# Unit pipeline of a top-k attention with a feed-forward block: P@V, scores, transpose, sine and gate at other places in each step

## The chip, the cores and the metric

The kernel runs on one core of one Trainium2 chip. The metric is the device time in microseconds (us) of one execution; a span is the same time as the profiler sees it. The engines that appear below are TensorE (PE, with its weight loads as PEld), VectorE (DVE), ScalarE (ACT), GpSimd (POOL) and SyncE (SP, which here only issues transfers).

## The reference

Attention over 8 batches x 8 heads, 576 positions, head size 64, in float32. Each row of scores keeps its 32 largest entries, and only these enter the softmax. The result, with the heads side by side, is the input of a feed-forward layer with 4608 tokens, width 512 and inner width 2048.

```python
scores = scale * np.matmul(q, k.transpose(0, 1, 3, 2))      # q, k, v: (8, 8, 576, 64)
kth = np.partition(scores, -32, axis=-1)[..., -32:-31]
scores = np.where(scores >= kth, scores, -1000000000.0)
scores = scores - np.max(scores, axis=-1, keepdims=True)
attn = np.exp(scores)
attn = attn / (np.sum(attn, axis=-1, keepdims=True) + 1e-09)
x = np.matmul(attn, v)             # then (B, H, S, D) -> (B*S, H*D): (4608, 512)
h = x @ w_in                       # w_in: (512, 2048)
g = h * np.cos(h)
out = g @ w_out                    # w_out: (2048, 512)
```

## The kernel before

The work is cut into 144 **units**: a unit is 128 tokens and one pair of heads (`hp`, 0 to 3). Four units make a **block** of 128 tokens, so there are 36 blocks. A batch has 576 tokens, which is 4.5 blocks; every ninth block therefore lies across two batches, and its units have two parts. The constants are `NP = 4`, `NU = 144`, `NF = 16`, `NC = 4`.

A unit goes through these stages, on different engines: scores (PE), copy out of PSUM (ACT), top-32 by four rounds of MAX8 and MATCH_REPLACE8 (DVE), mask and exponentials (ACT), reciprocal (DVE), normalise (POOL), split of the 32-bit words into two 16-bit halves (POOL), a write of the halves to DRAM and a transposing transfer back (SP), P@V (PE), and a copy to `xT` (ACT). The program is one Python loop; its step `i` emits one stage each of several neighbouring units, and every engine runs its own instructions in the order in which they were emitted. I call one pass of that loop a **step**. The two weight matrices arrive as 64-bit floats and are turned into 32-bit ones on ACT, DVE and POOL during the first steps (`load_weights`, `decode_first` to `decode_third`). Steps 0 to 8 are `early_slot`, 9 to 140 are `slot`, 141 to 144 are `last_slot`.

The feed-forward part of a finished block is woven into the steps in small portions: a block has 8 **first portions** (`ff1`, x @ w_in, 16 matmul instructions each) and 8 **second portions** (`ff2`, g @ w_out, 4 matmul instructions each). For each half block of h the cosine is made by a reduction (POOL), a sine (ACT) and a product called the gate (POOL). Whether a portion may be emitted is decided in Python by counters:

```python
    def can_first():
        if not first:
            return False
        blk, i = first[0]
        if blk["left"] or ff["tick"] < blk["tick"] + 2 or wq["ready"] < (((i + 1) * (256 // blk["w"]) - 1) // FC + 1) * NC:
            return False
        return i % 4 > 0 or ff["live"] + staged() < CHUNKS

    def can_second():
        if not second:
            return False
        blk, i, f = second[0]
        lag = 3 if 5 * NP < ff["now"] < NU - NP else 2
        gated = sum(ff["tick"] >= t + lag for t in blk["gated"])
        return gated * 1024 // blk["w"] >= f + 2 and wq["ready"] >= NC * NF // FC + f + 2

    def feed(n):
        ff["tick"] += 1
        while n > 0 and ff["credit"] >= 1:
            for kind in (ff["kind"], 1 - ff["kind"]):
                if (can_first, can_second)[kind]():
                    break
            else:
                return
            if kind == 0:
                ff1(*first.popleft())
            else:
                ff2(*second.popleft())
            if kind != ff["kind"] or ff["half"]:
                ff["kind"], ff["half"] = 1 - kind, 0
            else:
                ff["half"] = 1
            n, ff["credit"] = n - 1, ff["credit"] - 1
```

The stages that the change moves:

```python
    def write_halves(u):
        rows = u["rows"] = dram.tile([P, 2, 2 * S], U16, tag="rows", name="rows")
        nc.sync.dma_start(out=rows, in_=u.pop("halves"))

    def transposes(u):
        rows = u.pop("rows").rearrange("q h k -> (q h) k")
        pT = u["pT"] = work.tile([P, 2 * NT + 1, P], F32, tag="pT", name="pT", bufs=3)
        words = pT.rearrange("p c q -> p (c q)").bitcast(U16)
        nc.sync.dma_start_transpose(
            out=words.rearrange("p (c q) -> p c q", c=2 * NT + 1), in_=rows
        )

    # ... (cut)

    def take_values(us):
        blk, hp, n = block_of[us[0]["tok"]], us[0]["hp"], len(us)
        if "xT" not in blk:
            blk["xT"] = work.tile([P, NP, P], F32, tag="xT", name="xT", bufs=5)
        nc.scalar.copy(
            out=blk["xT"][:, hp : hp + n].rearrange("p h q -> p (h q)"),
            in_=room[0][:, 0 : n * P],
        )
        blk["left"] -= n
        blk["tick"] = ff["tick"]

    # ... (cut)

    def reduce_second():
        if not fresh or len(fresh[0]) < 3:
            return
        blk, g, x = fresh.popleft()
        if not ff["end"]:
            nc.gpsimd.tensor_tensor(out=x, in0=g, in1=x, op=ALU.subtract)
        waiting.append((blk, g, x, ff["now"], -TWO_PI_BELOW if ff["end"] else TWO_PI_BELOW))

    def sines(least):
        n = sum(c[3] < ff["now"] for c in waiting)
        if n == 0 or (n < least and waiting[0][3] + 2 > ff["now"]):
            return
        for _ in range(n):
            blk, g, x, _, scale = waiting.popleft()
            nc.scalar.activation(out=x, in_=x, func=AF.Sin, bias=halfpi, scale=scale)
            sined.append((blk, g, x))

    def gate(n):
        for _ in range(min(n, len(sined))):
            blk, g, x = sined.popleft()
            eng = nc.vector if ff["end"] else nc.gpsimd
            eng.tensor_tensor(out=g, in0=g, in1=x, op=ALU.mult)
            blk["gated"].append(ff["tick"])
```

The step of the middle of the run. `u` is unit i (top-k), `w` unit i-1 (mask, exponentials), `x` unit i-2 (reciprocal to write), `y` unit i-3 (transpose), `z` a pair of units whose P@V is made:

```python
    def slot(i, u, w, x, y, z):
        if x:
            reciprocal(x)
        if u:
            topk_first(u, w)
            decode_second(2)
        if u:
            topk_round(u, 1)
            topk_round(u, 2)
            topk_round(u, 3)
        if z:
            values(z)
        made = scored.get(i, [])
        if z:
            take_banks()
        else:
            feed(1)
        for m in made:
            scores(m)
        late = len(made) > 0
        if w:
            bounds(w)
            mask(w)
        take_banks()
        if w and late:
            exponentials(w)
        if z:
            take_values(z)
        take_scores(units[i + 1])
        if w and not late:
            exponentials(w)
        for load, b, hp in at_slot.get(i, []):
            load(b, hp)
        load_weights(2)
        if y:
            transposes(y)
        gate(1)
        if x:
            normalise(x)
            split(x)
            write_halves(x)
        feed(2)
        take_banks()
        decode_third()
        decode_first(2)
        reduce_first()
        reduce_second()
        feed(1 if len(made) == 2 else 3)
        if i % 2:
            sines(1)
        elif i < EARLY + 8 or i > LAST - 2:
            sines(2)
```

Which step makes whose scores and loads, and the loop:

```python
    EARLY, LAST = 2 * NP, NU - NP
    scored, last, last_values = {}, {}, {}
    for i, u in enumerate(units):
        two = i % 2 and EARLY + 2 < i < LAST + 2 and len(u["parts"]) == 1
        scored.setdefault(i - 2 if two else i - 1, []).append(u)
        for part in u["parts"]:
            last[part[0], u["hp"]] = i - 2 if two else i - 1
            last_values[part[0], u["hp"]] = i
    at_slot = {}
    order = [(b, hp) for b in range(B) for hp in range(NP)]
    for n in range(NP, len(order)):
        i = last[order[n - 5]] if n >= 5 else 0
        at_slot.setdefault(max(i, NP + 2), []).append((load_qk, *order[n]))
        i = last_values[order[n - 6]] if n >= 6 else 0
        at_slot.setdefault(max(i + 5 - i % 2, NP + 2), []).append((load_v, *order[n]))
    for hp in range(NP):
    # ... (cut)
    for i in range(NU + 1):
        ff["end"] = i >= NU
        ff["credit"] = min(ff["credit"] + 5.0 - 0.9 * len(scored.get(i, [])), 5.3)
        ff["now"] += 1
        wq["ready"] = wq["done"]
        u, w = (units[i - n] if 0 <= i - n < NU else None for n in range(2))
        x, y = (units[i - n] if EARLY <= i - n < LAST else None for n in range(2, 4))
        z = units[i - 5 : i - 3] if i % 2 and EARLY <= i - 5 < LAST else None
        if i <= EARLY:
            early_slot(i, u, w)
        elif i <= LAST:
            slot(i, u, w, x, y, z)
        else:
            last_slot(i, u, w, x, y, z)
    while first or second or full:
        ff["now"] += 1
        # ... (cut)
```

Of the kernel before, what the change touches and what calls it, by code (L numbers as in the profile page):

```python
# [31 lines left out]
def kernel(  # L32
# [16 lines left out]
    NP = H // 2  # L49
# [35 lines left out]
    for i in range(DF // CW):  # L85
        w = consts.tile([P, NC, CW], F32, tag=f"w_in{i}", name=f"w_in{i}")
# [4 lines left out]
    for f in range(NF):  # L91
        w = consts.tile([P, DM], F32, tag=f"w_out{f}", name=f"w_out{f}")
# [3 lines left out]
    ff = {"live": 0, "tick": 0, "now": 0, "credit": 0.0, "end": False, "kind": 0, "half": 0, "open": 0}  # L96
# [58 lines left out]
    units = []  # L155
    for t0 in range(0, B * S, P):
        parts = []
# [8 lines left out]
    NU = len(units)  # L166
# [174 lines left out]
    def reciprocal(u):  # L341
        u["rden"] = small.tile([P, 2], F32, tag="rden", name="rden")
        nc.vector.reciprocal(u["rden"], u.pop("den"))  # L343
# [19 lines left out]
# [11 lines that stand above are left out]
# [17 lines left out]
    def values(us):  # L391


        o = room[0]
        for i, u in enumerate(us):
            pT = u.pop("pT")
            for b, _, rows, r0 in u["parts"]:
                st = pairs[b, u["hp"]]
                r = slice(r0, r0 + rows)
                to = slice(i * P + r0, i * P + r0 + rows)  # L400
                for c in range(NT + 1):
                    for j in range(2):
                        d = slice(j * D, (j + 1) * D)
                        if c < NT:
                            lhsT, rhs = st["v"][:, c, d], pT[:, j * (NT + 1) + c, r]
                        else:
                            lhsT, rhs = st["v_tail"][:, d], pT[:, NT, r]
                        nc.tensor.matmul(o[d, to], lhsT, rhs, start=c == 0, stop=c == NT)  # L408
# [73 lines left out]
    def take_banks():  # L482
        while full:
            take, *what = full.popleft()
            take(*what)
# [30 lines left out]
# [16 lines that stand above are left out]
# [36 lines left out]
    def can_second():  # L568
        if not second:
            return False  # L570
        blk, i, f = second[0]

        lag = 3 if 5 * NP < ff["now"] < NU - NP else 2
        gated = sum(ff["tick"] >= t + lag for t in blk["gated"])
        return gated * 1024 // blk["w"] >= f + 2 and wq["ready"] >= NC * NF // FC + f + 2

# [18 lines that stand above are left out]
# [8 lines left out]
    EARLY, LAST = 2 * NP, NU - NP  # L603
    scored, last, last_values = {}, {}, {}
    for i, u in enumerate(units):
        two = i % 2 and EARLY + 2 < i < LAST + 2 and len(u["parts"]) == 1
        scored.setdefault(i - 2 if two else i - 1, []).append(u)
        for part in u["parts"]:
            last[part[0], u["hp"]] = i - 2 if two else i - 1
# [4 lines that stand above are left out]
        i = last[order[n - 5]] if n >= 5 else 0  # L614
        at_slot.setdefault(max(i, NP + 2), []).append((load_qk, *order[n]))
        i = last_values[order[n - 6]] if n >= 6 else 0
        at_slot.setdefault(max(i + 5 - i % 2, NP + 2), []).append((load_v, *order[n]))

    for hp in range(NP):
        at_slot.setdefault(hp, []).append((load_v, 0, hp))  # L620
# [44 lines left out]
        feed(2)  # L665
        sines(2)

    def slot(i, u, w, x, y, z):
        if x:
            reciprocal(x)  # L670
        if u:
# [3 lines that stand above are left out]
            topk_round(u, 1)  # L675
            topk_round(u, 2)
            topk_round(u, 3)
        if z:
            values(z)
        made = scored.get(i, [])  # L680
        if z:
            take_banks()
        else:
            feed(1)
        for m in made:
            scores(m)


        late = len(made) > 0
        if w:  # L690
            bounds(w)
            mask(w)
# [8 lines that stand above are left out]
        for load, b, hp in at_slot.get(i, []):  # L701
            load(b, hp)
        load_weights(2)
        if y:
            transposes(y)
        gate(1)
        if x:
            normalise(x)
            split(x)
            write_halves(x)  # L710
        feed(2)
        take_banks()
        decode_third()
        decode_first(2)
        reduce_first()
        reduce_second()
        feed(1 if len(made) == 2 else 3)
        if i % 2:
            sines(1)
        elif i < EARLY + 8 or i > LAST - 2:  # L720
            sines(2)

    def last_slot(i, u, w, x, y, z):
        if x:
            reciprocal(x)
        if u:
# [9 lines that stand above are left out]
        if i + 1 < NU:  # L736
            scores(units[i + 1])
        if z:
            take_values(z)
        if i + 1 < NU:  # L740
            take_scores(units[i + 1])
        if y:
            transposes(y)
        if x:
            normalise(x)
            split(x)
            write_halves(x)
        reciprocal(w)
        normalise(w)
        if u:  # L750
            topk_round(u, 2)
            topk_round(u, 3)
        gate(2)
        feed(2)
        transposes_now(w)
# [4 lines that stand above are left out]
        values([w])  # L760
        take_values([w])
        feed(2)
# [10 lines left out]
# [3 lines that stand above are left out]
        ff["now"] += 1  # L776
        wq["ready"] = wq["done"]
        u, w = (units[i - n] if 0 <= i - n < NU else None for n in range(2))
        x, y = (units[i - n] if EARLY <= i - n < LAST else None for n in range(2, 4))
        z = units[i - 5 : i - 3] if i % 2 and EARLY <= i - 5 < LAST else None  # L780
        if i <= EARLY:
            early_slot(i, u, w)
        elif i <= LAST:
            slot(i, u, w, x, y, z)
        else:
            last_slot(i, u, w, x, y, z)
    while first or second or full:
        ff["now"] += 1
        ff["credit"] = 2.0
# [44 lines left out]
```

## Time and profile before

| | |
|---|---|
| time, median of 3 | 1523.82 us (1522.76 to 1524.04) |
| span of the profiled execution | 1521.9 us |
| PE matmul / PE weight load busy | 1417.3 us (93%) / 1020.5 us (67%) |
| DVE busy | 1416.0 us (93%) |
| ACT busy | 1149.2 us (76%) |
| POOL busy | 1102.9 us (72%) |
| mean transfer rate | 139 GB/s |

The table gives each engine's busy time over the whole span. It can't be read as a single limit, because the run has stages: until about 200 us the feed-forward weights are still being decoded, then a long regular middle follows, and from about 1400 us the last units and the feed-forward work that is left. The profile also has a view by stretches of time, a list of waits (who stood idle, and what released it), and a timeline, in which an engine's instructions stand in order with the idle time before each and its releaser. "L465" is line 465 of the kernel; the lines that matter are L304 and L307 (top-k), L465 (first portions), L543 (second portions), L408 (P@V), L220 (scores), L348 and L360 (normalise, split), L365 and L371 (write, transpose), L504 to L513 (reduction), L523 (sine) and L530 (gate).

### The profile page before, as it was taken

How to read it: one execution, taken by the hardware profiler on the slowest of the kernel's cores; microseconds unless marked ns; L12 is line 12 of the kernel's file. 1: busy time of each engine (PE TensorE's matmuls, PEld its weight loads, DVE VectorE, ACT ScalarE, POOL GpSimd, SP SyncE). 2: the span in 40 equal slices, each digit the busy share in tenths (PEclk: the TensorE clock that was granted, in tenths of full speed). 3: DMA queues.
4: the chain of work that ended last, by engine and by line, in shares of the span. 5: the costliest groups of instructions: out<-in, count | busy, mean ns of one | idle time of the engine just before them, and what ended most of it. 6: DMA issues, size and time to landing. Idle time of an engine off the chain costs nothing.

```text
span 1521.9 us, 30207 instructions
## 1 busy us (share of the span) xinstructions
PE 1417.3 (93%) x10360; PEld 1020.5 (67%) x10360; DVE 1416.0 (93%) x4690; ACT 1149.2 (76%) x2322; POOL 1102.9 (72%) x837
## 2 busy tenths in 40 slices
PE   4567798999999999999999999999999999999899
PEld 3365365676777767777777767777777767776774
DVE  7989999999999999999999999999999999999521
ACT  7888766777777778877777777777777777777631
POOL 4777966778777778777777777777777777776500
PEclk6587999999999999999999999999999999999899
DMA  8422364645655555646655456555664455545000
GB/s 265 139 83 83 99 178 135 186 117 175 161 169 132 132 148 164 179 132 156 165 170 132 132 151 168 171 133 152 167 171 132 132 151 158 151 132 132 17 15 14
DMA packets 371753, 212.20 MB, mean 139 GB/s; under 512 B 321296, under 2 KB 337936, under 8 KB 371600
## 3 DMA queue, kind: packets, MB, share of 16 engines
q1 hardware_dynamic: 366192, 200.63, 48.7%
q10 hardware_dynamic: 5408, 9.65, 1.9%
q8 instruction: 81, 1.33, 0.4%
q14 instruction: 72, 0.59, 0.1%
HBM read 45.09 MB, written 87.29 MB: 87 GB/s over the span
## 4 chain that ended last, share of the span: by engine, by line
DVE 74%; PE 12%; ACT 6%; issue 3%; POOL 2%; DMA 2%; SPq 1%; DVEq 0%; ACTq 0%; POOLq 0%
DVE top L304 33%; DVE rest L307 27%; DVE rest L244 11%; PE o L543 5%; PE mm L465 4%; PE rim L408 2%; ACT s L334 1%; DVE top L292 1%; ACT s L326 1%; DVE top L297 1%; DVE w_out L138 1%; PE sc L220 1%; DMA pT<-rows 1%; DVE rden L343 1%; ACT st L127 1%
## 5 line engine op out<-in xcount | busy, mean ns | idle before, releaser
L304 DVE MAX8 top<-rest 128x8 f32<-128x288 f32 (+1 forms) x1656 | 681.2, 460 | 0.0
L465 PEld LDWEIGHTS mm<-xT,w_in 128*128 128x128 f32 x4608 | 536.3, 193 | 83.4 <-ACT g L478 39.8
L465 PE MATMUL mm<-xT,w_in 128*128 128x128 f32 x4608 | 546.9, 277 | 7.4 <-ACT g L478 3.4
L543 PE MATMUL o<-w_out,g 128*128 128x512 f32 x1152 | 532.1, 605 | 11.3 <-POOL g L530 5.6
L307 DVE MATCH_REPLACE8 rest<-top,rest 128x288 f32<-128x288 f32 (+1 forms) x1104 | 494.6, 455 | 0.0
L348 POOL TENSOR_SCALAR s<-s,rden 128x576 f32<-128x576 f32 x288 | 212.7, 750 | 259.1 <-DVE rden L343 259.1
L543 PEld LDWEIGHTS o<-w_out,g 128*128 128x128 f32 x1152 | 209.3, 192 | 232.4 <-issue 210.4
L360 POOL COPY halves<-s 128x2304 uint16<-128x2304 uint16 x132 | 277.7, 2103 | 27.4 <-DMA rows<-halves 19.9
L334 ACT ACTIVATE s<-s,nd 128x576 f32<-128x576 f32 x288 | 219.7, 764 | 0.8
L244 DVE TENSOR_TENSOR rest<-sc,s 128x576 f32<-128x576 f32 x264 | 198.5, 752 | 10.2 <-ACT s L231 2.7
L326 ACT ACTIVATE s<-s,nb 128x576 f32<-128x576 f32 x288 | 205.3, 760 | 0.0
L314 ACT ACTIVATE nb<-top 128x4 f32<-128x4 f32 x144 | 29.6, 206 | 230.2 <-DVE top L297 229.6
L408 PE MATMUL rim<-pT,v 128*64 128x128 f32 (+1 forms) x2560 | 163.1, 272 | 21.5 <-ACT pT L389 13.7
L530 POOL TENSOR_TENSOR g<-g,x 128x1024 f32<-128x1024 f32 x67 | 158.3, 2363 | 22.3 <-ACT nb L314 11.4
L220 PE MATMUL sc<-k,q 64*128 64x448 f32 (+1 forms) x640 | 150.1, 583 | 17.0 <-DMA k<-in_k_dram 9.3
L513 POOL TENSOR_TENSOR x<-g,x 128x1024 f32<-128x1024 f32 x68 | 161.0, 2367 | 5.7
L408 PEld LDWEIGHTS rim<-pT,v 128*64 128x64 f32 x2560 | 134.4, 141 | 38.3 <-ACT pT L389 16.3
L230 ACT COPY s<-sc 128x896 f32<-128x896 f32 x144 | 129.0, 896 | 3.3 <-PE sc L220 3.3
L478 ACT ACTIVATE g<-mm 128x512 f32<-128x512 f32 x144 | 83.7, 583 | 54.3 <-PE mm L465 43.9
L220 PEld LDWEIGHTS rim<-k,q 64*128 64x128 f32 (+1 forms) x640 | 57.3, 180 | 57.8 <-issue 52.7
L523 ACT ACTIVATE x<-x,halfpi 128x1024 f32<-128x1024 f32 x72 | 82.5, 1149 | 6.9 <-DVE x L499 6.1
L523 ACT ACT_TABLE_LOAD x66 | 84.7, 1283 | 1.6 <-ACT ob L553 0.4
(55 smaller groups left out, 1232.0 us busy)
## 6 DMA issues: line engine op xcount, KB each, us to landing
rows<-halves SPq DMA_DIRECT2D x132, 576.0 KB, 3.2
out_dram<-ob ACTq DMA_DIRECT2D x36, 256.0 KB, 2.9
q<-in_q_dram SPq DMA_DIRECT2D x31, 288.0 KB, 3.3
st<-in_moe_w_in_dram SPq DMA_DIRECT2D x16, 512.0 KB, 5.8
v<-in_v_dram SPq DMA_DIRECT2D x32, 256.0 KB, 3.9
st<-in_moe_w_out_dram SPq DMA_DIRECT2D x16, 512.0 KB, 3.6
k<-in_k_dram SPq DMA_DIRECT2D x31, 144.0 KB, 3.4
k<-in_k_dram SPq DMA_DIRECT2D x32, 128.0 KB, 3.8
```

Source lines behind the costliest of these rows:

```text
L220: nc.tensor.matmul(to[r0 : r0 + rows, j, 0 : k1 - k0], st["q"][d, q0 : q0 + rows], st["k"][d, k0:k1], start=True, stop=True,)
L244: nc.vector.tensor_tensor(out=u["rest"][:, :, i * HS : (i + 1) * HS], in0=sc[:, :, 0:HS], in1=s[:, :, HS:S], op=op,)
L304: nc.vector.max(to[:, j], src[:, j])
L307: nc.vector.match_replace(rest[:, j], to[:, j], src[:, j], NEG)
L326: nc.scalar.activation(out=s[:, j], in_=s[:, j], func=AF.Prelu, bias=nb[:, j, 1:2], scale=SCALE, alpha=FAR)
L334: nc.scalar.activation(out=s[:, j], in_=s[:, j], func=AF.Exp, bias=nd[:, j : j + 1], scale=1.0, accum_out=den[:, j : j + 1],)
L348: nc.gpsimd.tensor_scalar(out=s[:, j], in0=s[:, j], scalar1=rden[:, j : j + 1], scalar2=1.0, op0=ALU.mult, op1=ALU.mult,)
L360: nc.gpsimd.tensor_copy(out=halves, in_=s.rearrange("p (k h) -> p h k", h=2))
L408: nc.tensor.matmul(o[d, to], lhsT, rhs, start=c == 0, stop=c == NT)
L465: nc.tensor.matmul(mm[:, at : at + w], w_in[f // FC][:, c, (f % FC) * P : (f % FC + 1) * P], blk["xT"][:, c], start=c == 0, stop=c == NC - 1,)
L523: nc.scalar.activation(out=x, in_=x, func=AF.Sin, bias=halfpi, scale=scale)
L543: nc.tensor.matmul(o, g[:, at : at + P], w_out[f], start=f == 0, stop=f == NF - 1)
```

## The change

The change re-times the stages against each other; it adds no arithmetic and takes none away.

- P@V and the scores of two units were both emitted in odd steps; now both are in even steps. A pair's P@V (units 2k and 2k+1) moves from step 2k+5 to step 2k+4, and one feed-forward portion is emitted ahead of it.
- The transpose of a unit was emitted in the step after its write; now it directly follows the write in the same step.
- The sine was emitted at the end of odd steps; now it stands at the head of odd steps, ahead of the mask of that step.
- The gate was emitted ahead of normalise and split; now it comes behind them.
- The age in ticks that a gate must have before a second portion may use it is 3 from step 12 on, where it was 3 from step 20 on.
- The loads of v are emitted one step earlier, and units of head pair 0 that lie across two batches also get their scores one step earlier.

It is meant to shorten the way of a unit from top-k to the feed-forward part.

```diff
--- before.py
+++ after.py
@@ -570,7 +570,7 @@
             return False
         blk, i, f = second[0]
 
-        lag = 3 if 5 * NP < ff["now"] < NU - NP else 2
+        lag = 3 if 3 * NP < ff["now"] < NU - NP else 2
         gated = sum(ff["tick"] >= t + lag for t in blk["gated"])
         return gated * 1024 // blk["w"] >= f + 2 and wq["ready"] >= NC * NF // FC + f + 2
 
@@ -603,7 +603,7 @@
     EARLY, LAST = 2 * NP, NU - NP
     scored, last, last_values = {}, {}, {}
     for i, u in enumerate(units):
-        two = i % 2 and EARLY + 2 < i < LAST + 2 and len(u["parts"]) == 1
+        two = i % 2 == 0 and EARLY + 2 < i < LAST + 2 and (len(u["parts"]) == 1 or u["hp"] == 0)
         scored.setdefault(i - 2 if two else i - 1, []).append(u)
         for part in u["parts"]:
             last[part[0], u["hp"]] = i - 2 if two else i - 1
@@ -614,7 +614,7 @@
         i = last[order[n - 5]] if n >= 5 else 0
         at_slot.setdefault(max(i, NP + 2), []).append((load_qk, *order[n]))
         i = last_values[order[n - 6]] if n >= 6 else 0
-        at_slot.setdefault(max(i + 5 - i % 2, NP + 2), []).append((load_v, *order[n]))
+        at_slot.setdefault(max(i + 4 - i % 2, NP + 2), []).append((load_v, *order[n]))
 
     for hp in range(NP):
         at_slot.setdefault(hp, []).append((load_v, 0, hp))
@@ -665,7 +665,7 @@
         feed(2)
         sines(2)
 
-    def slot(i, u, w, x, y, z):
+    def slot(i, u, w, x, z):
         if x:
             reciprocal(x)
         if u:
@@ -675,18 +675,19 @@
             topk_round(u, 1)
             topk_round(u, 2)
             topk_round(u, 3)
-        if z:
-            values(z)
         made = scored.get(i, [])
         if z:
             take_banks()
-        else:
-            feed(1)
+        feed(1)
+        if z:
+            values(z)
         for m in made:
             scores(m)
 
 
         late = len(made) > 0
+        if i % 2:
+            sines(1)
         if w:
             bounds(w)
             mask(w)
@@ -701,26 +702,23 @@
         for load, b, hp in at_slot.get(i, []):
             load(b, hp)
         load_weights(2)
-        if y:
-            transposes(y)
-        gate(1)
         if x:
             normalise(x)
             split(x)
             write_halves(x)
-        feed(2)
+            transposes(x)
+        gate(1)
+        feed(1 if len(made) == 2 else 2)
         take_banks()
         decode_third()
         decode_first(2)
         reduce_first()
         reduce_second()
         feed(1 if len(made) == 2 else 3)
-        if i % 2:
+        if i < EARLY + 4 or i == LAST:
             sines(1)
-        elif i < EARLY + 8 or i > LAST - 2:
-            sines(2)
-
-    def last_slot(i, u, w, x, y, z):
+
+    def last_slot(i, u, w, x, z):
         if x:
             reciprocal(x)
         if u:
@@ -739,12 +737,11 @@
             take_values(z)
         if i + 1 < NU:
             take_scores(units[i + 1])
-        if y:
-            transposes(y)
         if x:
             normalise(x)
             split(x)
             write_halves(x)
+            transposes(x)
         reciprocal(w)
         normalise(w)
         if u:
@@ -776,14 +773,14 @@
         ff["now"] += 1
         wq["ready"] = wq["done"]
         u, w = (units[i - n] if 0 <= i - n < NU else None for n in range(2))
-        x, y = (units[i - n] if EARLY <= i - n < LAST else None for n in range(2, 4))
-        z = units[i - 5 : i - 3] if i % 2 and EARLY <= i - 5 < LAST else None
+        x = units[i - 2] if EARLY <= i - 2 < LAST else None
+        z = units[i - 4 : i - 2] if i % 2 == 0 and EARLY <= i - 4 < LAST else None
         if i <= EARLY:
             early_slot(i, u, w)
         elif i <= LAST:
-            slot(i, u, w, x, y, z)
+            slot(i, u, w, x, z)
         else:
-            last_slot(i, u, w, x, y, z)
+            last_slot(i, u, w, x, z)
     while first or second or full:
         ff["now"] += 1
         ff["credit"] = 2.0
```

## The prediction

> **What bounds the kernel now.** I read the page first: busy times, then the 40 slices.
>
> ```profile
> PE 1417.3 (93%) x10360; PEld 1020.5 (67%) x10360; DVE 1416.0 (93%) x4690; ACT 1149.2 (76%) x2322; POOL 1102.9 (72%) x837
> ...
> PE   4567798999999999999999999999999999999899
> DVE  7989999999999999999999999999999999999521
> ```
>
> Two engines are full, but not at the same ends. PE starts slowly and works to the last slice; DVE is full early and empty in the last three slices (a slice is 38 us). The view by stretches (us; then busy PE, PEld, DVE, ACT, POOL with counts, clock, DMA share, GB/s) says the same in numbers:
>
> ```profile
> 500.00:700.00 200.00, 197.77 (x1562) 143.82 (x1560) 198.86 (x695) 159.65 (x322) 155.47 (x116) 1.00 0.55 147
> 1400.00:1450.00 50.00, 44.06 (x305) 32.80 (x300) 30.14 (x81) 33.13 (x71) 25.00 (x21) 0.90 0.18 42
> 1450.00:1522.00 72.00, 68.13 (x345) 44.54 (x343) 13.80 (x13) 13.49 (x20) 0.03 (x1) 1.00 0.04 15
> ```
>
> In the middle a step lasts 9.51 us (reciprocals at 1390.79 and 1400.31 in the timeline) and DVE is busy 99.4% of it: DVE sets the pace there. After 1400 us DVE has little left and PE runs on. So the end is DVE's pace up to step 140 **plus the PE work still open then**. How much is open? The same view for L465 (ff1) and then for L543 (ff2) alone:
>
> ```profile
> 1400.00:1456.00 56.00, 18.65 (x128) 17.84 (x128) 0.91 0.17 42
> 1456.00:1522.00 66.00, 22.40 (x192) 22.38 (x192) 1.00 0.03 12
> ```
> ```profile
> 1400.00:1456.00 56.00, 15.48 (x34) 6.25 (x35) 0.91 0.17 42
> 1456.00:1522.00 66.00, 41.68 (x95) 17.22 (x93) 1.00 0.03 12
> ```
>
> An ff1 portion is 16 instructions, an ff2 portion 4. Open at 1400 us: 320/16 = 20 first and 129/4 = 32 second portions, 52 of 576. Of these 12 and 24 lie after the last P@V (1455.2 us). One portion costs (1518.1 - 1455.2)/36 = 1.75 us of PE there; two take 3.44 to 3.66 us in the middle. Only the last block's 16 must come after its P@V; the other 20 are backlog, 35 us of it. Backlog is what this change can shorten.
>
> **What the Trainium skill says.** "Perfetto Trace Analysis", section Identifying the Most-Contended Engine, warns that matmul busy share isn't a measure of PE's headroom. It agrees here in so far as "busy" PE hides waits: I therefore count PE work in portions. From its section Optimization Strategy I take that a kernel can have several regimes; this one has three. "DMA: Bandwidth & Descriptors", section Two DMAs through the same engine are not ordered, says that a dependent transfer has to wait for the first one's completion semaphore. The trace shows that wait: between 300 and 1395 us, SP's queue stood 238.4 us before transposes for their rows. "ScalarE: Activation LUTs", section What ACT_TABLE_LOAD costs, gives about 1283 ns for a load; the trace has 1283 ns, 66 before sines. The change doesn't alter how often sine and exponentials alternate (once in two steps), so I count nothing for it.
>
> **The change, part by part.**
>
> *P@V one step earlier.* A pair's P@V comes in step 2k+4 instead of 2k+5; a block is ready for ff1 a step, 9.5 us, earlier. The credit rule gives 5.0 - 0.9 per scored unit, capped at 5.3. In both kernels a step with two scored units can emit at most 3 portions (2+1 before, 1+1+1 after), a step with none emits 5; so 8 per two steps in both, which is exactly the demand (16 per block of four steps). PE work of two steps: 8 portions 14.2 us, two P@V 2.4, two scores 2.15, in sum 18.76 us of 19.02 (714.39 to 716.79 to 718.94 us in the timeline, and the four pairs of portions before). So the middle can't go faster, and backlog lost early is never made up: **its size at step 140 is decided in the steps before 32**.
>
> *Sine at the head, gate behind the split.* Before, a reduction emitted in odd step i isn't old enough for the sine at the end of i; it waits until i+2, and its gate until i+3. After, the reduction falls in even step i, the sine at the head of i+1, the gate in i+1. A gate comes about two steps sooner, so ff2 may follow sooner.
>
> *Counting it.* I stepped the counters of `feed` through all steps for both versions (credit, ticks, lag, weight readiness). Portions emitted by the end of a step:
>
> ```
> step      14  17  20  22  26  28  30  32  140
> before    31  40  50  56  72  78  84  92  524
> after     31  40  51  59  75  83  91  99  532
> ```
>
> The count before agrees with the trace (268 + 256 = 524 portions by 1400 us). What the older kernel loses: in step 27 only one portion is emitted, because the gate of the next ff2 is under 3 ticks old and the new block's ff1 isn't ready; in step 30, three instead of five. After, the wider lag costs an empty step 17, but from 18 on every pair of steps gives 8. By 32 the lead is 7, with the different rhythm of step 140 it is 8. Behind the last P@V 28 portions are left instead of 36. Saved: 8 x 1.75 = **14.0 us**. The last steps 141 to 144 (about 55 us, four or five portions each) I leave as they are.
>
> *Transpose issued with its write.* Per unit SP now waits about 3.2 us (median landing of a write) with its queue blocked, then 2.6 us of issue: 6.2 us with the write, of 9.5 us per step. In steps with eight q/k loads (about 4.6 us) that is 10.8, more than a step. From a normal odd step: split ends 3.9 us into it (1.5 normalise, 2.1 split), write landed at 7.1, transpose landed 4.8 us later at 11.9; PE begins an even step 0.8 us before DVE (714.39 against 715.17), then makes a portion (1.8) and the other unit's P@V (1.2), so it reaches that unit's P@V at 9.5 + 2.2 = 11.7. So PE may wait 0.2 us and a few us in load steps. Each shifts PE against DVE once; PE can run about 3.5 us later before the next unit's scores are late. Cost: 0 to 2 us at the end.
>
> *Start of the run.* Here POOL, full with weight decoding, is late:
>
> ```profile
> 186.97 1.47 POOL L348 TENSOR_SCALAR s<-s,rden 128x576 f32<-128x576 f32 x2
> 188.50 2.10 POOL L360 COPY halves<-s 128x2304 uint16<-128x2304 uint16 x1
> ```
> ```profile
> 194.47 2.57 SPq L371 DMA_TRANSPOSE pT<-rows  x1
> ```
>
> This is unit 11, whose reciprocal was at 178.61: normalise begins 8.4 us late, and the transpose, issued at 194.47, lands about 199. Before, its P@V comes in step 15 (198.34 us), just in time. After, it comes in step 14, which PE reaches near 190; POOL does the same work, so it still lands about 199. The scores of unit 15 stand behind that P@V, ready about 201.4, copied by ACT about 202.7; DVE wants them at 197.8. I expect a **DVE stall of about 5 us** once, which moves everything later. Some of the old start's waits (1.97 us of DVE for ACT's copy at 247 us) may go. Net +4 us.
>
> Sum: 1523.8 - 14.0 + 4 = 1513.8; with 0 to 2 us of PE waits, and 1 to 2 us back because P@V of two units leaves the last steps: **1513 us**.
>
> **Rivals.** *ACT's sine becomes a wait of each pair.* Look at one pair of steps (reduction, sine, end of the merge, bounds):
>
> ```profile
> 703.39 2.37 POOL L513 TENSOR_TENSOR x<-g,x 128x1024 f32<-128x1024 f32 x1
> ...
> 704.57 1.15 ACT L523 ACTIVATE x<-x,halfpi 128x1024 f32<-128x1024 f32 x1
> ...
> 707.33 0.18 DVE L297 TENSOR_REDUCE top<-top 128x2 f32<-128x34 f32 x1
> ...
> 707.55 0.21 ACT L314 ACTIVATE nb<-top 128x4 f32<-128x4 f32 x1 [1.83 <-DVE top L297]
> ```
>
> Here the sine is of an older reduction. After, it is the one just made: POOL ends it at 705.76, the sine would end at about 707.0, and the mask needs ACT at 707.5. It fits by half a microsecond; the exponentials of that step ended 0.76 us before DVE's next reciprocal (714.41, 715.17). A POOL delay over about 1.3 us would stall DVE, in each of some 60 pairs: 0.3 us each is 18 us, and the time is 1530. For it: the thin margin. Against: the gate no longer stands ahead of normalise, POOL rests over 3 us in odd steps, and ACT waits 198.4 us for DVE between 300 and 1395 us, 1.7 us each time.
>
> *SP becomes the bound*, if transposes pile up behind loads: each P@V then waits, scores behind it are late, DVE waits too. For it: the 10.8 us of a load step. Against: only three steps of the run load eight, and average SP use is about 7 us of 9.5. It would give 1520 to 1535.
>
> *Nothing is gained*, if PE simply idles where it had worked: then backlog doesn't shrink, and 1524 +- 3 results. Against it stands the count, which the trace of before confirms.
>
> **Range and chances.** The gain from the count alone with no stall at the start gives 1508; with the last steps shorter too, 1504. A stall of 5 us and PE waits give 1515; with the first rival in mild form, 1525. Range 1504 to 1525. Over 2% faster would be under 1493: it needs 17 portions, while only 20 are backlog; 3%. Over 2% slower is over 1554: half a microsecond of DVE per pair; 4%. Within 2%: 93%.
>
> **What would show it.** Right: L465 and L543 together have 28 portions after the last P@V; DVE stays over 99% busy in the middle; one DVE idle of 3 to 6 us for ACT's copy (L231) near 198 us. Wrong: reciprocals in the middle more than 9.55 us apart; DVE waiting for ACT's den (L339) or copy in each pair; P@V waiting for the transfer of pT by tens of us in sum; or as many portions left as before.

## The result and the profile after

The changed kernel takes 1541.92 us (median; 1539.52 to 1551.65) against 1523.29 us: a ratio of 1.0135, 95% interval 1.009 to 1.018. It is slower, by 18.6 us or 1.35%, and lies outside the predicted range.

The page after, the lines that answer to those shown of before (busy times, then tenths busy in 40 slices, each now 38.5 us):

```profile
PE 1419.2 (92%) x10360; PEld 1022.2 (66%) x10360; DVE 1419.5 (92%) x4689; ACT 1158.4 (75%) x2326; POOL 1104.3 (72%) x838
...
PE   4577787999999999999999999999999998999999
DVE  7989988999999998999899999999999998999831
```

Busy times are the same within 1%; the work didn't grow. DVE's row now has eights in the middle, where it was all nines. The view by stretches (us; then busy PE, PEld, DVE, ACT, POOL with counts, clock, DMA share, GB/s) sizes it:

```profile
500.00:700.00 200.00, 194.41 (x1497) 138.84 (x1494) 193.47 (x676) 154.86 (x310) 153.46 (x114) 0.99 0.52 147
1400.00:1450.00 50.00, 46.68 (x316) 33.73 (x315) 49.36 (x171) 37.87 (x79) 36.34 (x27) 0.97 0.45 128
1450.00:1541.00 91.00, 85.96 (x533) 59.69 (x531) 30.53 (x50) 35.32 (x68) 12.65 (x11) 1.00 0.03 12
```

Of the 200 us in the middle DVE is idle 6.5, where it was 1.1. The same view after the last P@V, for L465 and then for L543:

```profile
1487.00:1541.00 54.00, 18.67 (x160) 18.65 (x160) 1.00 0.04 15
```
```profile
1487.00:1541.00 54.00, 32.10 (x72) 13.22 (x72) 1.00 0.04 15
```

160/16 = 10 first and 72/4 = 18 second portions are left: 28, as counted, against 36 before. So the gain came, and something larger was lost. The reciprocal (L343) marks the start of each step on DVE; from its starts in the timeline:

| stretch | before, us | after, us | difference |
|---|---|---|---|
| to step 24 | 287.2 | 299.6 | +12.4 |
| steps 24 to 139 | 1103.6 | 1128.1 | +24.5 |
| step 140 | 9.5 | 9.5 | 0 |
| step 141 to the end of the span | 121.6 | 104.3 | -17.3 |

Between steps 24 and 139 nearly every step still takes 9.5 us; the 24.5 us lie in eleven steps: 35, 37, 55, 57, 71, 75, 91, 107, 111, 127 and 131 (up to 14.2 us). Eight of them come back at a distance of 36 steps, the length of two batches, as the loads of q, k and v do (35, 71 and 107; 55, 91 and 127; 75 and 111). The list of waits between 300 and 1395 us (who <- whom: us in all, times, longest), first for all engines, then SP's own queue:

```profile
POOL s L348 <- DVE rden L343: 163.4, 77, 4.7
...
ACT xT L414 <- PE rim L220: 116.1, 56, 7.2
...
POOL halves L360 <- DMA rows<-halves: 60.9, 30, 7.0
...
ACT nb L314 <- DVE top L297: 33.5, 52, 1.3
...
PE rim L408 <- DMA pT<-rows: 27.1, 19, 3.6
...
DVE rest L244 <- ACT s L231: 25.2, 11, 4.8
```
```profile
SPq L371 <- DMA rows<-halves: 309.0, 113, 4.6
...
SPq L185 <- PE rim L220: 98.5, 19, 7.1
```

ACT had waited 198.4 us for DVE's merge, its slack; now that is 33.5, and 116.1 us of waiting for PE stand in its place. PE waits 19 times for pT before a P@V, 27.1 us in all, where it was 2.9 us in five waits: this is one of the signs by which the prediction said that it would be wrong. DVE waits eleven times for the copy of the scores (L231), the eleven long steps. One of them, step 35, in the timeline (start, duration, engine, operation, idle before):

```profile
379.49 1.09 PE L408 MATMUL rim<-pT,v 128*64 128x128 f32 x16 [0.91 <-DMA pT<-rows]
...
382.02 0.34 SPq L185 DMA_DIRECT2D q<-in_q_dram  x1
...
386.70 1.36 SPq L365 DMA_DIRECT2D rows<-halves  x1
390.76 2.59 SPq L371 DMA_TRANSPOSE pT<-rows  x1
393.44 0.53 SPq L365 DMA_DIRECT2D rows<-halves  x1
...
394.73 0.15 DVE L343 RECIPROCAL rden<-den 128x2 f32<-128x2 f32 x1
...
395.35 1.98 PE L543 MATMUL o<-w_out,g 128*128 128x512 f32 x4
...
396.76 2.34 SPq L371 DMA_TRANSPOSE pT<-rows  x1
...
401.25 1.09 PE L408 MATMUL rim<-pT,v 128*64 128x128 f32 x16 [2.67 <-DMA pT<-rows]
402.17 0.53 PE L408 MATMUL rim<-pT,v_tail 128*64 128x128 f32 x4
402.63 1.86 PE L220 MATMUL sc<-k,q 64*128 64x448 f32 x4
...
406.39 0.37 ACT L414 COPY xT<-rim 128x256 f32<-128x256 f32 x1 [5.88 <-PE rim L220]
406.66 0.91 ACT L230 COPY s<-sc 128x896 f32<-128x896 f32 x1
...
407.88 0.76 DVE L244 TENSOR_TENSOR rest<-sc,s 128x576 f32<-128x576 f32 x1 [3.50 <-ACT s L231]
```

Read it downwards. SP waits for PE's scores, then issues eight loads of q and k, and only at 386.70 the write of a unit whose split had ended at 379.6 us. The next unit's split waits for that write to land (the halves have one buffer), so its write goes out at 393.44 and its transpose at 396.76. PE, which had already waited 0.91 us in step 32 and begins step 34 0.62 us after DVE (395.35 against 394.73), stands 2.67 us before that unit's P@V; both units' scores stand behind it; ACT's copy to xT waits for all of them, the copy of the scores stands behind that, and DVE waits 3.50 us.

### The profile page after: what moved, and what is told of

Its sections match the earlier page's. It is cut to its first block, busy times and chain, and to the rows that moved or that the text cites. A ratio compares the mean times of both kernels' runs of the same rounds, so it can differ in the third digit from the quotient of the medians.

```text
span 1541.6 us, 30172 instructions
## 1 busy us (share of the span) xinstructions
PE 1419.2 (92%) x10360; PEld 1022.2 (66%) x10360; DVE 1419.5 (92%) x4689; ACT 1158.4 (75%) x2326; POOL 1104.3 (72%) x838
## 4 chain that ended last, share of the span: by engine, by line
PE 41%; DVE 20%; DMA 16%; POOL 8%; ACT 6%; SPq 6%; issue 4%; ACTq 0%; POOLq 0%; DVEq 0%
PE o L543 14%; PE mm L465 14%; DMA rows<-halves 9%; DVE top L304 8%; DVE rest L307 7%; PE rim L408 7%; DMA pT<-rows 6%; PE sc L220 5%; DVE rest L244 3%; SPq L371 3%; POOL halves L360 2%; POOL s L348 2%; POOL x L513 2%; PE rim L220 1%; POOL g L530 1%
## 5 line engine op out<-in xcount | busy, mean ns | idle before, releaser
L465 PEld LDWEIGHTS mm<-xT,w_in 128*128 128x128 f32 x4608 | 543.0, 194 | 75.7 <-issue 61.1
L465 PE MATMUL mm<-xT,w_in 128*128 128x128 f32 x4608 | 546.0, 277 | 9.5 <-ACT g L478 9.5
L543 PE MATMUL o<-w_out,g 128*128 128x512 f32 x1152 | 540.2, 603 | 11.6 <-POOL g L530 5.6
L543 PEld LDWEIGHTS o<-w_out,g 128*128 128x128 f32 x1152 | 203.7, 191 | 201.5 <-issue 179.5
L244 DVE TENSOR_TENSOR rest<-sc,s 128x576 f32<-128x576 f32 x264 | 198.7, 753 | 39.0 <-ACT s L231 32.1
L408 PE MATMUL rim<-pT,v 128*64 128x128 f32 (+1 forms) x2560 | 167.4, 276 | 49.2 <-DMA pT<-rows 35.8
L220 PE MATMUL sc<-k,q 64*128 64x448 f32 (+1 forms) x640 | 153.1, 605 | 7.9 <-DMA k<-in_k_dram 7.9
L414 ACT COPY xT<-rim 128x256 f32<-128x256 f32 (+1 forms) x78 | 27.7, 355 | 148.2 <-PE rim L220 135.9
L220 PEld LDWEIGHTS rim<-k,q 64*128 64x128 f32 (+1 forms) x640 | 58.2, 186 | 61.2 <-issue 56.0
```

The lines of the kernel that those rows point to most:

```text
L220: nc.tensor.matmul(to[r0 : r0 + rows, j, 0 : k1 - k0], st["q"][d, q0 : q0 + rows], st["k"][d, k0:k1], start=True, stop=True,)
L244: nc.vector.tensor_tensor(out=u["rest"][:, :, i * HS : (i + 1) * HS], in0=sc[:, :, 0:HS], in1=s[:, :, HS:S], op=op,)
L465: nc.tensor.matmul(mm[:, at : at + w], w_in[f // FC][:, c, (f % FC) * P : (f % FC + 1) * P], blk["xT"][:, c], start=c == 0, stop=c == NC - 1,)
L543: nc.tensor.matmul(o, g[:, at : at + P], w_out[f], start=f == 0, stop=f == NF - 1)
```

## The experiments

**Theory A**: in SP's queue the loads stand ahead of the write and the transpose, so pT comes late and with it everything behind. **B**: write, landing and transpose are too long for a P@V in step 2k+4 anyway. **C**: the sine's wait for POOL holds up the exponentials. **D**, which joins A and B: the P@V one step earlier leaves the path split, write, transpose, P@V, scores, copy, DVE without slack. **E**: the loss at the start is due to sine and gate in the steps in which POOL is behind. In the tables "to 24", "middle" and "end" are the start of step 24, the time over 9.51 us per step in steps 24 to 139, and the time from step 141 to the end, from the profiled run (one execution, which can lie some us off the median); before has 287.2, 0.5 and 121.6, the changed kernel 299.6, 25.0 and 104.3.

**1. Loads behind the transpose, and loads one step later.** In the changed kernel, with the loads of the weights (`load_weights`, the last one at about 171 us) moved along:

```diff
-        for load, b, hp in at_slot.get(i, []):
-            load(b, hp)
-        load_weights(2)
         if x:
             normalise(x)
             split(x)
             write_halves(x)
             transposes(x)
+        for load, b, hp in at_slot.get(i, []):
+            load(b, hp)
+        load_weights(2)
```

> The changed kernel with the loads of q, k and v issued behind the write and the transpose of the same step. Theory A (SP's queue: the loads stand ahead of the write and the transpose, so pT and with it P@V, both units' scores and their copy come late): the 24.5 us of DVE idle in steps 35 to 131 and the 5.8 us of step 19 go, time about 1512 us. Theory B (write, landing and transpose alone are too long for a P@V in step 2k+4, loads or not): the stalls stay, 1538 to 1542 us. Theory C (the sine's wait for POOL holds the exponentials): the same, 1538 to 1542 us.

For the second the order stays, but q and k of an even step are loaded in the next one, where nothing needs them sooner:

```diff
-        at_slot.setdefault(max(i, NP + 2), []).append((load_qk, *order[n]))
+        i = max(i, NP + 2)
+        # ... (cut: first_use is the first step that scores with it)
+        if i > EARLY and i % 2 == 0 and first_use > i + 1:
+            i += 1
+        at_slot.setdefault(i, []).append((load_qk, *order[n]))
```

> The changed kernel with the q and k loads of even steps issued one step later, where the buffer has been free for some time; order within a step unchanged. Theory A in its narrower form (SP stands before these loads because PE's scores still read the buffer, 98.5 us in all, and holds the write): most of the 24.5 us of DVE idle go, 1517 to 1522 us. If it is the mere number of issues in SP's queue, wherever they stand: 1530 to 1540 us.

| | us | ratio to before | to 24 | middle | end |
|---|---|---|---|---|---|
| loads behind | 1519.49 | 0.9987 (0.9974 to 0.9999) | 292.0 | 8.5 | 104.5 |
| loads later | 1526.96 | 1.0036 (1.002 to 1.0051) | 293.5 | 12.3 | 104.5 |

DVE's waits in the run with the loads behind, over the whole span:

```profile
DVE rest L244 <- ACT s L231: 8.6, 5, 3.5
```

It was 32.1 us in 14 waits in the changed kernel. Moving three lines took back 22.4 us: A holds for two thirds of the middle and for the long step 19. B as the only cause falls, and so does C for the middle, since neither was touched. About half is due to SP waiting for PE before q and k alone, as the second run shows. Both came out above what A had expected (about 1512, and 1517 to 1522 us): a third of the middle's loss is left, and P@V still waits 12.0 us for pT between 300 and 1395 us.

**2. All loads in odd steps, and the sine of the start back.** The first of these puts the loads behind the transpose and moves both q, k and v from even to odd steps (of its edit, the part for v):

```diff
-        at_slot.setdefault(max(i + 4 - i % 2, NP + 2), []).append((load_v, *order[n]))
+        i = max(i + 4 - i % 2, NP + 2)
+        at_slot.setdefault(i + 1 if i > EARLY else i, []).append((load_v, *order[n]))
```

> The changed kernel with all loads behind the transpose, and the loads of even steps moved to the odd step after (except q and k that the next step needs). Theory A: what is left of DVE idle in the middle with loads merely behind the transpose (8.5 us, steps 95 to 131) comes from v loads that run into the next write; it falls to 3 us or less, time 1512 to 1515 us. If the residue has another cause (P@V ahead of the scores, with the transposes' own spread): 1517 to 1520 us.

The second also puts the sine at the end of odd steps under 16:

```diff
-        if i % 2:
+        if i % 2 and i >= 16:
             sines(1)
 ...
-        if i < EARLY + 4 or i == LAST:
+        if i % 2 and i < 16 or i == LAST:
             sines(1)
```

> As the run before, and in steps under 16 the sine stands at the end of odd steps again. The counters give the same 532 portions by the end of step 140. Theory C, which I hold for the start alone: the 8.5 us for which ACT waits there for POOL's reduction, and the 3.9 us of DVE behind it in step 13, go; 3 to 4 us less than the run before, 1508 to 1512 us. If PE's P@V then waits for the same late POOL instead, no gain.

| | us | ratio to before | to 24 | middle | end |
|---|---|---|---|---|---|
| loads in odd steps | 1517.67 | 0.9964 (0.9953 to 0.9975) | 291.6 | 7.1 | 102.9 |
| and sine of the start | 1521.27 | 0.9995 (0.9986 to 1.0004) | 298.5 | 7.8 | 104.5 |

The first is a little faster than before. The middle's rest hardly fell, to 7.1 us, but it has another cause now. P@V waits for pT only 3.4 us between 300 and 1395 us, 0.7 us at most, and no long step follows such a wait. Three of its four long steps (59, 95 and 131, where DVE waits 1.08, 3.25 and 1.78 us) follow a P@V across two batches that waits for v, which this run loads a step later (0.63, 1.95 and 1.44 us). Step 95:

```profile
964.19 0.69 PE L408 MATMUL rim<-pT,v 128*64 128x64 f32 x16 [1.95 <-DMA v<-in_v_dram]
...
971.41 0.76 DVE L244 TENSOR_TENSOR rest<-sc,s 128x576 f32<-128x576 f32 x1 [3.25 <-ACT s L231]
```

The fourth, step 127 with 0.61 us, has no such wait ahead of it and stays open. So with the loads out of pT's way its waits no longer reach DVE, which speaks for A in nearly all of the middle; the edit put a late v in their place. In the second DVE's 4 us wait for the exponentials in step 13 did go, but one of 4.05 us came at the end of step 12, after ACT had waited 8.65 us for the last load of the weights, which stands behind the transpose in this run too. At 211 us DVE waited 5.52 us for the copy of the scores, after PE had waited 6.08 us for pT, as the alternative in the expectation had it. The sine's place in the start isn't settled by this run.

**3. The sine at the end of even steps.** In the changed kernel:

```diff
-        if i % 2:
-            sines(1)
 ...
-        if i < EARLY + 4 or i == LAST:
+        if i % 2 == 0 or i < EARLY + 4:
             sines(1)
```

> The changed kernel with the sine put back to the end of the steps that have scores (even ones). By the counters 528 portions lie before the end of step 140 instead of 532, 4 x 1.75 = 7 us more at the end. Theory C in the start of the run (the sine of step 13 waits 8.5 us for POOL and the exponentials, then DVE's reciprocal, 3.9 us): that wait goes. Theory A: the middle keeps its 24.5 us. Sum about 1545 us. If theory C held in the middle too: under 1525 us.

Measured: 1571.91 us, ratio 1.033 (1.0305 to 1.0356); to 24 300.1, middle 47.7, end 111.1. A miss of 27 us. The end is as counted (four portions more, 111.1 - 104.3 = 6.8 us), and the wait in step 13 is gone; but the start is no better and the middle's stalls nearly doubled. They are the same waits (DVE for the copy, PE for pT 45.0 us between 250 and 1395 us); why more of them was not tested further. It shows that the middle's stalls don't need the sine at the head.

**4. One number in the old kernel.** I wanted the worth of open portions alone:

```diff
-        lag = 3 if 5 * NP < ff["now"] < NU - NP else 2
+        lag = 2
```

> The kernel before with one number changed: a gate may be used by a second portion after 2 ticks everywhere. By the counters 530 portions lie before the end of step 140 instead of 524, nothing else moves. If open portions set the end at 1.75 us each: 6 x 1.75 = 10.5 us less, 1513 us. If the younger gates make PE wait for POOL instead, PE waits for g (L530) grow and the time is 1520 or more.

Measured: 1592.94 us, ratio 1.0466 (1.0446 to 1.0485); middle 84.7, end 108.5. This missed by 80 us. The end did shrink, by 13.1 us, but the younger gates gave the portions another rhythm in which, between 250 and 1395 us, POOL waits 146.9 us for ACT's copies of h (56 times) and DVE 75.5 us for the exponentials' sums. "Nothing else moves" was wrong: the counters move the order on every engine.

**5. The gate ahead again, and the transpose alone.** The changed kernel with one line moved:

```diff
+        gate(1)
         if x:
             normalise(x)
             split(x)
             write_halves(x)
             transposes(x)
-        gate(1)
```

> The changed kernel with the gate ahead of normalise and split again. In odd steps normalise, split, write and transpose start 2.4 us later. Theory D (pT of the odd unit is on a path that has no slack: split, write, landing, transpose, P@V, scores, copy, DVE): DVE waits for the copy in many pairs, 0.5 us or more each, 1560 us or more. If pT has slack outside load steps: within 5 us of the changed kernel, 1537 to 1547.

And the kernel before, with the transpose of a unit directly behind its write (in `slot` and in `last_slot`), P@V where it was:

```diff
-        if y:
-            transposes(y)
         gate(1)
         if x:
             normalise(x)
             split(x)
             write_halves(x)
+            transposes(x)
```

> The kernel before with one part of the change alone: the transpose directly behind its write, P@V still in step 2k+5. Theory D: with one more step of slack nothing waits for pT, the longer hold of SP's queue is harmless: 1521 to 1526 us. If holding SP is harmful by itself (loads of q and k come late, PE waits for them): 1530 us or more.

| | us | ratio to before | to 24 | middle | end |
|---|---|---|---|---|---|
| gate ahead | 1712.64 | 1.1247 (1.123 to 1.1263) | 311.9 | 183.9 | 104.9 |
| transpose alone | 1520.11 | 0.9993 (0.9984 to 1.0003) | 284.7 | 0.6 | 118.7 |

The waits of the run with the gate ahead, 300 to 1395 us:

```profile
ACT xT L414 <- PE rim L220: 264.4, 50, 9.1
POOL g L530 <- ACT x L523: 258.5, 50, 8.9
DVE rest L244 <- ACT s L231: 162.7, 50, 7.3
```

Fifty times each, one for every pair of steps: a closed ring. The gate waits for the sine, normalise and split stand behind the gate, pT comes late, so do P@V, scores and copy, and the next sine stands behind that copy on ACT. So in the changed kernel the place of the gate behind the split is not an extra, it is what keeps this ring open: every delay of the odd unit's pT goes straight to DVE. That is theory D. With one step more of slack, the second run, SP's longer hold costs nothing.

**6. Everything but the move of P@V.** The kernel before with the transpose behind its write, the gate behind the split, and the sine at the head of the step after the scores (even ones here); P@V stays in step 2k+5, scores in odd steps. With P@V stay what goes with its move: the loads of v, the portion ahead of it, the earlier scores across two batches, and the wider lag from step 20 on. The second run has the loads behind the transpose as well, as in 1. In `last_slot` the transpose moves as in 5.

```diff
         late = len(made) > 0
+        if i % 2 == 0:
+            sines(1)
 ...
-        if y:
-            transposes(y)
-        gate(1)
         if x:
             normalise(x)
             split(x)
             write_halves(x)
+            transposes(x)
+        gate(1)
 ...
-        if i % 2:
+        if i < EARLY + 4 or i == LAST:
             sines(1)
-        elif i < EARLY + 8 or i > LAST - 2:
-            sines(2)
```

> The kernel before with the transpose behind its write, the gate behind the split and the sine at the head of the step after the scores (even steps here), but P@V and scores where they were (P@V in step 2k+5, scores in odd steps). The counters give 528 portions by the end of step 140, 4 more than before. Theory D (the loss is the P@V without slack behind pT): DVE stays at 9.5 us per step, 4 x 1.75 = 7 us less than before, 1514 to 1517 us. If sine at the head or gate behind the split stall DVE by themselves: DVE waits for den (L339), 1530 us or more.

> As the run before, with the loads of q, k and v behind the write and the transpose of the step. With a step of slack for pT the place of the loads shouldn't matter: within 2 us of the run before. If SP's queue costs something even then: 3 to 5 us less.

| | us | ratio to before | to 24 | middle | end |
|---|---|---|---|---|---|
| all but P@V | 1520.24 | 0.9986 (0.9978 to 0.9993) | 296.6 | 0.6 | 109.3 |
| loads behind as well | 1530.52 | 1.006 (1.0043 to 1.0077) | 304.3 | 2.1 | 107.7 |

The middle is clean again: the move of P@V, with what goes with it, is what the 24.5 us hang on. Yet the time stayed 3 us above the expected range, because to step 24 another 9.4 us are lost although P@V didn't move. With the loads behind, it is worse by 10 us, not the same: 7.7 us of it are lost before step 24 (304.3 against 296.6), and after that PE waits for k (4.2 us, its weight loads 5.4 us, between 250 and 1395 us). Part of the loss before step 24 comes from the weights, whose last load goes out at 171.5 us instead of 155.7 us:

```profile
171.50 0.53 SPq L116 DMA_DIRECT2D st<-in_moe_w_out_dram  x1
...
175.47 0.66 ACT L126 ACTIVATE w_out<-st 128x512 f32<-128x512 f32 x1 [8.64 <-DMA st<-in_moe_w_out_dram]
```

DVE then waits 5.10 us for the exponentials' sum at the end of step 12, which gets 2.7 us longer; the other 5 us lie in steps 16 and 22 and weren't traced to a cause. So the place that saved 22 us in the changed kernel costs 10 here, but how much of that is due to q, k and v isn't shown: no run moved them without the weights.

**7. The new order from step 24 on.** This keeps the old order of sine and gate while the weights are being decoded. The second run has the gate ahead of normalise in all steps. In `last_slot` the transpose moves as in 5.

```diff
+        if i >= 24 and i % 2 == 0:       # ahead of bounds(w)
+            sines(1)
 ...
-        if y:
-            transposes(y)
-        gate(1)
+        if i < 24:
+            gate(1)
         if x:
             normalise(x)
             split(x)
             write_halves(x)
+            transposes(x)
+        if i >= 24:
+            gate(1)
 ...
-        if i % 2:
+        if i < 24 and i % 2 or i == LAST:
             sines(1)
-        elif i < EARLY + 8 or i > LAST - 2:
+        elif i < EARLY + 8:
             sines(2)
```

> Transpose behind its write everywhere, P@V in step 2k+5, and the sine at the head of even steps and the gate behind the split only from step 24 on; before that both as in the kernel before. The counters still give 528 portions by the end of step 140. Theory E (what the parts without the P@V move gain at the end, about 12 us, was lost again by waits for POOL in the steps under 24, 9.4 us): start like before, end like the run with all parts but the P@V move, 1509 to 1513 us. If the late start is due to something else in the change (the transposes): 1518 to 1521 us.

> As the run before, with the gate ahead of normalise and split in all steps. Theory D (the gate's place is costly only where P@V has no slack behind pT): within 3 us of the run before. If the ring sine, gate, normalise, split is itself the loop: DVE waits for den or the copy in many steps, 1530 us or more.

| | us | ratio to before | to 24 | middle | end |
|---|---|---|---|---|---|
| from step 24 on | 1509.06 | 0.9908 (0.9895 to 0.9922) | 285.7 | 0.6 | 108.9 |
| with the gate ahead | 1510.40 | 0.9921 (0.9909 to 0.9933) | 286.4 | 0.6 | 108.9 |

This beats both kernels. From its list of DVE's waits over the whole span:

```profile
DVE rest L244 <- ACT s L231: 2.3, 2, 1.5
```

E holds: start like before, end like the run of 6. And the gate's place, worth 171 us where P@V had no slack (1712.64 - 1541.92), is worth 1.3 us where it has a step.

## Why the prediction was wrong

**The count was right.** 28 portions were left, as predicted, and the end fell by 17.3 us; the prediction had 14.0, and 1 to 2 for the last steps. That the middle sets the pace by DVE and that backlog is decided before step 32 held too.

**The step that failed first is "Transpose issued with its write".** It had the right chain and the right margin (pT lands within 0.2 us of when PE wants it), and then said "Each shifts PE against DVE once" and "Cost: 0 to 2 us at the end". The runs show 24.5 us there. Two things were wrong. Firstly, the shift is not made once. SP waited for PE before the q and k loads in the kernel before too (78.2 us, up to 6.2 at a time, between 300 and 1395 us), when pT was not yet tight (P@V waited 2.9 us for it in all); now it waits 98.5 us, up to 7.1, and a pT without slack stands behind. A late PE so makes the next pT later still, and PE has 0.26 us per pair of steps to catch up. The run with the loads behind takes back two thirds of it, and with the loads in odd steps no wait for pT reaches DVE. Secondly, PE didn't have the 3.5 us in hand: I had let ACT's copy of the first unit's scores begin when those scores are made, but the xT copy stands ahead of it on ACT and waits for both units' scores, about 1 us later. In the timelines of the middle the copy of the scores (L231) ends 2.4 to 2.6 us before DVE's L244 begins in every pair of the kernel before, and 0 to 1.8 us before it in the changed one. The order was to be seen before: its trace has the same release, `ACT xT L414 <- PE rim L220`, 4.6 us in two waits.

The prediction also left out what a wait does to PE's clock. The five steps with the longest excess (35, 55, 71, 107 and 127, 18.6 of the 24.5 us) follow the five longest waits for pT, and after each of these the granted clock fell (last section), which made both units' scores later still.

**The second is "Start of the run"**, +4 us net, measured +12.4. The DVE stall near 198 us came (3.94 us) but it waited for the exponentials' sum, not for the copy: ACT's sine had waited 8.46 us for POOL. That is the first rival, which I had weighed for the middle only. A further 6.9 us were waits for the copy, in steps 19 (5.80 us, the SP mechanism again), 18 (0.83) and 15 (0.27), and 1.07 us for the exponentials' sum ended step 11. Of the 12.4 us the loads behind the transpose take back 7.6 (to step 24: 292.0), the waits for the copy among them; they leave the sine's wait. The run with all parts but P@V loses 9.4 us to step 24, in part in other steps, and the run with the transpose alone none: there sine and gate account for it, and taking them out of the start removes it. About 4 us of the changed kernel's loss lie in four decoding instructions on DVE that ran longer (L137 1.88 us for 0.41 us in step 10; L137 0.83, L138 2.20 and 1.40 for 0.42, 0.85 and 0.77 in step 12); what lengthened them was not tried.

**The rivals.** "SP becomes the bound, if transposes pile up behind loads" named the mechanism. I set it aside because only three steps load eight tiles and because SP's average use is below a step; but an average says nothing of a queue that waits in order. The first rival came once, at the start. **Open** is whether the move of P@V can be had without the loss: no run emitted the scores ahead of P@V or the copy to xT behind that of the scores, and none combined the move, from step 24 on, with loads that come neither ahead of pT nor too late for v.

## What to carry to other kernels

Before a stage is pulled forward, write down the whole path to the bound engine, with each copy that stands ahead of the needed one in its engine's order, and ask for slack in the worst step: the load step, the step across batches, the steps of the start. In SP's queue here a load that waited up to 7.1 us for its buffer held the writes and transposes behind it, so the queue's mean use, below a step, was no measure of its delay. If a re-timing gains at one end and loses at the other, keep the parts that gain and apply them only from the step on where the engine they lean on has time: here leaving P@V where it was turned +1.35% into -0.1%, and starting sine and gate at step 24 turned that into -0.9%.

## What the runs showed of the hardware that I had not expected

PE's granted clock fell right after short waits. In step 34 the wait for pT lasted 2.67 us; in the view by stretches the clock is then:

```profile
401.00:402.00 1.00, 0.76 (x14) 0.76 (x16) 1.00 (x4) 0.00 (x0) 0.92 (x2) 1.00 0.00 0
402.00:404.00 2.00, 2.00 (x16) 1.16 (x12) 2.00 (x9) 0.00 (x0) 1.92 (x2) 0.57 0.00 0
404.00:406.00 2.00, 2.00 (x12) 1.11 (x10) 0.38 (x2) 0.00 (x0) 2.00 (x3) 0.58 0.03 7
```

For about 4 us PE ran at 0.57 of full speed, and the scores that DVE waited for took 1.86 us instead of 1.02. The Trainium skill's "TensorE: Matmul & The Clock Gate", section "HAM oscillation — how this bites in real kernels", speaks of idle gaps over about 3.4 us; here the clock fell after a wait of 2.67 us. Four us at 0.57 are some 1.7 us of work lost besides the wait itself, an estimate from these three lines. Of the 19 waits for pT between 300 and 1395 us, the five of 2.44 to 3.58 us were followed by 2 us or more at 0.50 to 0.66; after the other fourteen, up to 1.78 us, the clock stood at 1.00. In the run with loads in odd steps a wait of 1.95 us was followed by 0.50. What PE had done ahead of the wait was not varied, so this is no rule for other kernels.
